# Half-width loads for two FFN weight slices, one PSUM bank for both tokens of a pair, and a new load order

## The chip, the cores and the metric

The kernel runs on one core of a Trainium2 chip. The metric is the device time of one execution in microseconds; of several executions the median is taken. TensorE (PE) does the matrix products and the transposes, VectorE (DVE), ScalarE (ACT) and GpSimd (POOL) do the elementwise work, and SyncE (SP) issues every DMA of this kernel.

## The reference

```python
state = np.zeros((B, H, D, D))            # B=4, H=8, S=768, D=64
for t in range(S):
    state = gamma[None, :, None, None] * state + np.einsum('bhd,bhe->bhde', k[:, :, t], v[:, :, t])
    y[:, :, t] = scale * np.einsum('bhd,bhde->bhe', q[:, :, t], state)
x = y.transpose(0, 2, 1, 3).reshape(B * S, H * D)     # 3072 x 512
h = np.maximum(x @ w_in, 0.0)                         # w_in: 512 x 2048
out = h * h @ w_out                                   # w_out: 2048 x 512, out in float32
```

It is a retention recurrence with one decay per head, followed by a feed-forward network (FFN) with a squared ReLU.

## The kernel before

The 3072 tokens are worked in 24 tiles of 128 tokens, numbered m, six for each batch. For each tile the recurrence is done in chunked form in two halves of 64 tokens ("sub"): scores of k and q (`scores`, L566), sums of k and v (`sums`, L577), a causal mask on DVE (L620), the running state on DVE (L631, L633), then `values` (L540) and `apply` (L555), and a scaled copy into the FFN input `xt` (L642). The decay is folded into tables that scale v and y. A call `visit(m, n)` (L581) issues values and apply of tile m and scores and sums of tile n in one piece on TensorE. In this text "scores n" is the scores and sums of tile n, and "apply m" is values and apply of tile m.

Scores need k and q transposed. Before the change this is done in four ways:

- Tiles 0 to 3 come in pairs (`together`, L397): one DMA of 512 KB for each of k, q and v brings 256 tokens, with neighbouring tokens g = 0 and 1 on one partition. The casts (L411, POOL, ACT or DVE) write bf16 "twins" that lie in an FFN buffer named h. For each g and each of k and q, four transposes (L430) go into a PSUM bank of their own, and one copy takes the bank out for both tiles, into every second column. Rows of k and v are brought into token order by matmuls with a permutation (L449, "placing") and copied out of PSUM.
- Tiles 4 to 6 (below `NPE`) are loaded singly (L470, 256 KB each), cast (L476), and transposed with four 128x128 transposes for each of k and q (L523), which are called a transpose side here.
- Tiles 7 to 9 (`NPE` to `NTD`) are transposed by `flips`, 32 transposes of 64x64 into spare columns of the PSUM tile `yy` (L496), and one copy of 1024 elements on ACT (L502).
- Tiles 10 to 23 are transposed by a DMA that SP issues (L514, called X with the tile's number).

The FFN takes blocks of 1, 2 or 4 tiles (`BLOCKS`). `ffn1` (L663) multiplies with `w_in`, held in four slices of 512 columns, in groups that fill one PSUM bank (L680, 512 columns in all), then ReLU on ACT (L685) and the square on DVE (L690). `ffn2` (L705) multiplies with `w_out`, held in four slices of 512 rows, four matmuls of 512 columns for each slice (L724), then a copy on ACT (L732) and a store of 256 KB on SP (L736). Each weight slice comes in one DMA of 1 MB into one of four float32 buffers `wst` (`weights`, L649), and four casts (L657) on whichever of DVE, ACT and POOL the planner picks write it as bf16. w_out slices reuse the buffers of the w_in slices.

The order of all work on each engine is made ahead of time by a planner (`Plan.schedule`, L65). Each operation is given engines, costs, data it reads and writes, and a priority; the planner puts them down one after the other and chooses the earliest start, then the lowest priority value. The emitted order is fixed: on the chip each engine works through its queue in order, and an instruction that waits holds back what stands behind it. Loads are ranked by the string `ORDER` (L219). Four PSUM banks (`fps`) are handed out by the planner with "open", "use" and "close". It also emits 40 tiny matmuls at the start (`PRE`) and filler matmuls (L776) where it expects TensorE to be idle around `WARM`.

The planner's order of loads before the change, in full up to the weights' end: k0 v0 q0 k2 v2 w_in0 q2 w_in1 q4 w_in2 k4 w_in3 w_out0 k5 w_out1 v4 q5 w_out2 q6 v5 v6 w_out3 q7 k6 k7 v7.

Of the kernel before, what the change touches and what calls it, by code (L numbers as in the profile page):

```python
# [11 lines left out]
BF16 = mybir.dt.bfloat16  # L12
# [6 lines left out]
class Plan:  # L19
# [45 lines left out]
    def schedule(self, nbanks, max_open):  # L65
        ops = self.ops
        n = len(ops)
# [7 lines left out]
        end = [None] * n  # L75
# [10 lines left out]
        bank_free = [0.0] * (nbanks - 1) + [WARM + 1]  # L86
        bank_of = {}
        open_groups = set()
        pipe = made = 0.0
        late = []  # L90
        outstanding = {e: [] for e in eng_free}
# [2 lines left out]
        while done < n:  # L94
            best = None
            for eng, cand in pool.items():
                ef = eng_free[eng]
                for i in cand:
                    o = ops[i]
                    t = max(ef, ready_at[i])  # L100
                    b = o["bank"]
# [69 lines left out]
                eng_free[eng] = t + dur  # L171
                end[i] = t + dur + o["lat"]
            if b is not None and b[0] == "close":
                bank_free[bank_of[b[1]]] = end[i]
                open_groups.discard(b[1])
            if b is not None:
                o["bank_index"] = bank_of[b[1]]
            done += 1
# [9 lines left out]


SMALL = (1.20, 0.93, 65, 0.6)  # L190
TWIN = (1.20, 1.75, 65, 0.6)
TURN = (0.60, 1.10, 16, 2.4)
WIDE = (0.60, 2.80, 33, 0.6)
STORE = (0.30, 0.80, 9, 0.6)
BLOCKS = [2, 1, 1, 1, 1, 2, 4, 2, 2, 4, 4]
SPLIT = 6
AHEAD = 4
WARM = 14.0
FILL = 0.215
WARMING = 5.5  # L200
PACE = 6
LEAD = 2
NPE = 7
NTD = 10
PRE = 40
CVT = {'DVE': 0.69, 'POOL': 1.1}
TCAST = {'DVE': 0.43, 'ACT': 0.63, 'POOL': 0.78}
TEVAC = {'ACT': 0.6, 'DVE': 0.62}
MEVAC = {'ACT': 0.6}
NPAIR = 2  # L210
F2LAG = 3.0
F2WAIT = 4
# [4 lines left out]


ORDER = (  # L219
    "k0 v0 q0 k2 v2 i0 q2 i1 q4 i2 o0 o1 k4 i3 k5 v4 q5 o2 q6 v5 v6 o3 q7 k6 k7 v7"  # L220
)


# [8 lines left out]
def kernel(  # L232
# [164 lines left out]
    def together(n):  # L397


        b, i = where(2 * n)  # L400
        m, s0, w, twin = 2 * n, (2 * n) % NLD, n % 2, twins[n % 2]
        rows_ = lambda x: ld[x][:, s0 : s0 + 2, :].rearrange("s u n -> s (u n)")
        held = lambda x: (f"ld{x}{s0}", f"ld{x}{s0 + 1}")
        for x in "kqv":
            pl.add(f"ld{x}{m}", "SP", TWIN, (), held(x),
                   lambda x=x: nc.sync.dma_start(  # L406
                       rows_(x).rearrange("s (h n) -> s h n", h=H),
                       src[x][b, :, i * C : (i + 2) * C, :].rearrange("h (s g) d -> s h (g d)", g=2)),
                   prio=dma_prio[(x, m)])
        for g in range(2):  # L410
            for x in "kq":  # L411
                o = twin[x][:, g, :].rearrange("s (j a d) -> s a j d", a=2, j=NJ)
                t = rows_(x).rearrange("s (a j g d) -> s a j g d", a=2, j=NJ, g=2)[:, :, :, g, :]
                pl.add(f"c{x}{m}.{g}", TCAST, 0, held(x), (f"twin{x}{w}.{g}",),
                       lambda on, t=t, o=o: copy_on(on, o, t), prio=urgency(m))
            t = rows_("v").rearrange("s (h g d) -> s h g d", h=H, g=2)[:, :, g, :]
            pl.add(f"cv{m}.{g}", CVT, 0, held("v") + ("vf2",), (f"twinv{w}.{g}",),
                   lambda on, t=t, g=g: (nc.vector if on == "DVE" else nc.gpsimd).tensor_tensor(
                       out=twin["v"][:, g, :].rearrange("s (h d) -> s h d", h=H), in0=t,
                       in1=vf2[:, i // 2, g, :, None].to_broadcast([P, H, D]), op=ALU.mult),  # L420
                   prio=urgency(m))
        q0 = m % NQT
        for g in range(2):
            for x, name in enumerate("kq"):
                o1 = {}

                def turn_fn(x=x, name=name, g=g, o1=o1):
                    ps = fps[o1["op"]["bank_index"]].bitcast(BF16)
                    for j in range(NJ):
                        nc.tensor.transpose(ps[:, j * P : j * P + P], twin[name][:, g, j * P : j * P + P], ident[:])  # L430
                i0 = pl.add(f"T{name}{m}.{g}", "PE", 0.26, (f"twin{name}{w}.{g}", "ident"), (f"gT{name}{m}{g}",), turn_fn,
                            prio=-200 + m, lat=0.2, count=4, bank=("open", ("T", m, x, g), False))
                twin_users.append(i0)
                o1["op"] = pl.ops[i0]
                pl.add(f"E{name}{m}.{g}", TEVAC, 0, (f"gT{name}{m}{g}",),
                       (f"qkT{q0}.{name}{g}", f"qkT{q0 + 1}.{name}{g}"),
                       lambda on, x=x, g=g, o1=o1: copy_on(
                           on, qkt_all[:, q0 : q0 + 2, x].rearrange("p c j (t g) -> p c j t g", g=2)[:, :, :, :, g],
                           fps[o1["op"]["bank_index"]].bitcast(BF16)[:, 0:512].rearrange("p (j c t) -> p c j t", j=NJ, c=2)),
                       prio=urgency(m), lat=0.05, bank=("close", ("T", m, x, g)))  # L440
        for c in range(2):
            r = slice(L * c, L * c + L)
            for name in "kv":
                o1 = {}

                def place(name=name, r=r, o1=o1):
                    ps = fps[o1["op"]["bank_index"]]
                    for g in range(2):
                        nc.tensor.matmul(ps[:], lhsT=perm[r, g, :], rhs=twin[name][r, g, :], start=(g == 0), stop=(g == 1))  # L449
                i0 = pl.add(f"N{name}{m + c}", "PE", 0.45, (f"twin{name}{w}.0", f"twin{name}{w}.1", "perm"), (f"gN{name}{m + c}",),  # L450
                            place, prio=-190 + m + c, lat=0.2, count=2, bank=("open", ("N", m + c, name), False))
                twin_users.append(i0)
                o1["op"] = pl.ops[i0]
                o = bf[name][(m + c) % NBF]
                o = o.rearrange("s j a d -> s (j a d)") if name == "k" else o.rearrange("s h d -> s (h d)")
                pl.add(f"M{name}{m + c}", MEVAC, 0, (f"gN{name}{m + c}",), (f"bf{name}{(m + c) % NBF}",),
                       lambda on, o=o, o1=o1: copy_on(on, o, fps[o1["op"]["bank_index"]][:]),
                       prio=urgency(m + c), lat=0.05, bank=("close", ("N", m + c, name)))
# [25 lines left out]
               prio=urgency(m))  # L484

    def qkeys(m):
        return [f"qkT{m % NQT}.{x}{g}" for x in "kq" for g in range(2)]

    def flips(m):

# [15 lines left out]
    def transpose(m):  # L506
# [10 lines left out]
        for x, name in enumerate("kq"):  # L517
            o1 = {}

            def fn(x=x, o1=o1):  # L520
                ps = fps[o1["op"]["bank_index"]].bitcast(BF16)
                for j in range(NJ):
                    nc.tensor.transpose(ps[:, j * P : j * P + P], t[:, x, j].rearrange("s a d -> s (a d)"), ident[:])  # L523
            i0 = pl.add(f"T{name}{m}", "PE", 0.26, (f"bf{name}{m % NBF}", "ident"), (f"gT{name}{m}",), fn,
                        prio=-200 + m, lat=0.2, count=4, bank=("open", ("T", m, x), False))
            o1["op"] = pl.ops[i0]
            pl.add(f"E{name}{m}", EVAC, 0, (f"gT{name}{m}",), qkeys(m)[2 * x : 2 * x + 2],
                   lambda on, x=x, o1=o1: copy_on(on, qkT[:, x].rearrange("p j t -> p (j t)"),
                                                  fps[o1["op"]["bank_index"]].bitcast(BF16)[:, 0:512]),
                   prio=urgency(m), lat=0.05, bank=("close", ("T", m, x)))  # L530
# [115 lines left out]
                   prio=urgency(m))  # L646


    def weights(kind, j):  # L649
        slot = (j if kind == "in" else 4 + j) % NWS  # L650
        st = wst[slot]
        dst = w_in_bf[j] if kind == "in" else w_out_bf[j]
        wv = (moe_w_in.rearrange("(cb p) f -> p cb f", p=P)[:, :, j * 512 : (j + 1) * 512] if kind == "in"
              else moe_w_out.rearrange("(fb p) n -> p fb n", p=P)[:, 4 * j : 4 * j + 4, :])
        pl.add(f"ldw{kind}{j}", "SP", WIDE, (), (f"wst{slot}",),
               lambda: nc.sync.dma_start(st[:], wv), prio=dma_prio[(kind, j)])  # L656
        for c in range(4):  # L657
            pl.add(f"cw{kind}{j}.{c}", WCAST, 0, (f"wst{slot}",), (f"w{kind}{j}.{c}",),
                   lambda on, c=c: copy_on(on, dst[:, c, :], st[:, c, :]),
                   prio=WPRIO[kind] + j)  # L660


    def ffn1(blk):  # L663
# [5 lines left out]
        for f0 in range(0, NFB, per):  # L669
            grp = ("f1", blk, f0)  # L670
            j = f0 // 4
            reads = [f"xt{g % NXT}.{u0 + u}" for u in range(nb)] + [f"win{j}.{cb}" for cb in range(NCB)]
            o1 = {}

            def mm(f0=f0, j=j, o1=o1):
# [29 lines left out]
    def ffn2(blk):  # L705
        for q4 in range(blk0[blk], blk0[blk] + blocks[blk]):
# [5 lines left out]
            for part in range(parts):  # L712
# [2 lines left out]
                keys = [f"osb{slot}.{part}"] if parts > 1 else [f"osb{slot}.0", f"osb{slot}.1"]  # L715
                o1 = {}
                for j in range(4):
                    reads = [f"h{g % NH2}.{u}.{4 * j + c}" for c in range(4)] + [f"wout{j}.{c}" for c in range(4)]

                    def mm(j=j, o1=o1, h2=h2, u=u, ns=ns, w=w):  # L720
                        ps = fps[o1["op"]["bank_index"]]
# [16 lines left out]

    dma_prio = {x: n for n, x in enumerate(dma_order(NM))}
    urgency = lambda m: m - 3.0  # L740
    for j in range(4):
        weights("in", j)
    for j in range(4):
        weights("out", j)
    done = done2 = 0
    for m in range(-1, NM):
        n = m + 1
# [62 lines left out]
```

## Time and profile before

| what | value |
|---|---|
| median of 4 runs | 213.54 us (213.42 to 213.6) |
| the profiled execution | 213.49 us, span 211.6 us |
| mean granted TensorE clock | 0.992 |
| busy: PE, DVE, ACT, POOL | 200.4, 113.6, 94.5, 42.6 us |
| FFN input product (L680), FFN output product (L724) | 93.9 and 92.4 us busy |
| DMA moved | 37.64 MB, mean 178 GB/s |
| w_in slice, w_out slice, from issue to landing | 9.8 and 9.3 us (median) |

The span is the time from the first to the last instruction; the execution's own time is longer by what lies around it. Busy times of different engines overlap. The row of tenths on the page cuts the span into 40 slices of 5.29 us. Queries of the trace give the same execution in order of time; in brackets stands how long the engine sat idle before an instruction and what released it. When a load has landed is read from the first cast that it released.

### The profile page before, as it was taken

How to read it: one execution, taken by the hardware profiler on the slowest of the kernel's cores; microseconds unless marked ns; L12 is line 12 of the kernel's file. 1: busy time of each engine (PE TensorE's matmuls, PEld its weight loads, DVE VectorE, ACT ScalarE, POOL GpSimd, SP SyncE). 2: the span in 40 equal slices, each digit the busy share in tenths (PEclk: the TensorE clock that was granted, in tenths of full speed). 3: DMA queues.
4: the chain of work that ended last, by engine and by line, in shares of the span. 5: the costliest groups of instructions: out<-in, count | busy, mean ns of one | idle time of the engine just before them, and what ended most of it. 6: DMA issues, size and time to landing. Idle time of an engine off the chain costs nothing.

```text
span 211.6 us, 6380 instructions
## 1 busy us (share of the span) xinstructions
PE 200.4 (95%) x2788; PEld 119.1 (56%) x2788; DVE 113.6 (54%) x253; ACT 94.5 (45%) x157; POOL 42.6 (20%) x70
## 2 busy tenths in 40 slices
PE   2886999999999999999999999999999999999994
PEld 2344888675676755444566667644444444444453
DVE  3465889765577764367863753656463442322100
ACT  8675666544355521265334244223534324534321
POOL 6551423305233231232322121310000000000000
PEclk9997899999999999999999999999999999999999
DMA  6999999999999996999999999981011011011022
GB/s 166 290 343 343 348 352 247 296 299 201 264 233 205 215 224 156 253 203 230 156 240 203 210 245 201 235 181 63 0 53 50 3 50 50 3 51 50 0 102 99
DMA packets 91276, 37.64 MB, mean 178 GB/s; under 512 B 77808, under 2 KB 84208, under 8 KB 91248
## 3 DMA queue, kind: packets, MB, share of 16 engines
q1 hardware_dynamic: 91248, 37.23, 76.7%
q8 instruction: 22, 0.36, 0.7%
q14 instruction: 6, 0.05, 0.1%
HBM read 27.26 MB, written 6.29 MB: 159 GB/s over the span
## 4 chain that ended last, share of the span: by engine, by line
PE 88%; DMA 5%; SPq 3%; ACT 1%; DVE 1%; issue 0%
PE fps L680 40%; PE fps L724 38%; DMA qn<-in_q_dram 5%; SPq L406 3%; PE yy L540 2%; PE yy L555 2%; PE sc L566 2%; PE sc L577 1%; ACT qkT L502 1%; SPq L656 1%; PE fps L523 1%; DVE xt L642 1%; PE yy L496 1%; PE fps L430 0%; ACT h L388 0%
## 5 line engine op out<-in xcount | busy, mean ns | idle before, releaser
L680 PE MATMUL fps<-xt,w_in 128*128 128x256 bf16 (+2 forms) x704 | 93.9, 284 | 0.1
L724 PE MATMUL fps<-w_out,h 128*128 128x512 bf16 (+1 forms) x400 | 92.4, 371 | 0.0
L685 ACT ACTIVATE h<-fps 128x512 bf16<-128x512 f32 x96 | 57.2, 597 | 66.5 <-PE fps L680 66.3
L680 PEld LDWEIGHTS <-w_in 128*128 128x128 bf16 x704 | 58.6, 99 | 31.1 <-issue 0.7
L690 DVE TENSOR_TENSOR h<-h 128x512 bf16<-128x512 bf16 x96 | 42.0, 445 | 52.5 <-ACT h L685 51.9
L724 PEld LDWEIGHTS <-h 128*128 128x128 bf16 x400 | 37.5, 98 | 36.0
L732 ACT ACTIVATE osb<-fps 128x512 f32<-128x512 f32 (+1 forms) x25 | 14.5, 580 | 32.2 <-PE fps L724 28.6
L642 DVE TENSOR_TENSOR xt<-yy,yf 128x512 bf16<-128x512 f32 x24 | 16.5, 688 | 17.2 <-PE yy L555 12.8
L392 POOL CAST kqs<-kn 128x512 bf16<-128x512 f32 x19 | 13.0, 687 | 54.4 <-DMA kn<-in_k_dram 44.5
L620 DVE TENSOR_TENSOR pt<-sc,cmask 128x512 bf16<-128x512 f32 x24 | 16.4, 682 | 2.2 <-PE sc L577 2.2
L633 DVE TENSOR_TENSOR state<-sc,state 128x256 bf16<-128x256 f32 x40 | 16.8, 419 | 0.6
L392 POOL CAST kqs<-qn 128x512 bf16<-128x512 f32 x20 | 13.3, 666 | 15.0 <-DMA qn<-in_q_dram 14.9
L481 DVE TENSOR_TENSOR vs<-vn,vf 128x512 bf16<-128x512 f32 x20 | 14.1, 706 | 0.8 <-DMA vn<-in_v_dram 0.8
L555 PE MATMUL yy<-qkT,state 64*64 64x64 bf16 x352 | 12.1, 198 | 0.8 <-DVE state L633 0.3
L540 PEld LDWEIGHTS <-vs 64*64 64x64 bf16 x384 | 5.1, 107 | 7.5 <-issue 7.3
L430 PE MATMUL fps<-ident,h 128*128 128x128 bf16 x32 | 3.9, 284 | 5.2 <-DVE h L390 3.5
L555 PEld LDWEIGHTS <-state 64*64 64x64 bf16 x352 | 7.4, 106 | 1.6 <-PE yy L555 1.1
L540 PE MATMUL yy<-pt,vs 64*64 64x64 bf16 x384 | 7.6, 197 | 0.6 <-DVE pt L620 0.6
L566 PE MATMUL sc<-qkT 64*64 64x64 bf16 x384 | 7.7, 198 | 0.0
L577 PE MATMUL sc<-vs,kqs 64*64 64x64 bf16 x352 | 7.7, 196 | 0.0
L388 ACT ACTIVATE qkT<-fps 128x512 bf16<-128x512 bf16 x7 | 4.8, 698 | 5.6 <-PE fps L523 3.5
L390 DVE COPY qkT<-fps 128x512 bf16<-128x512 bf16 x7 | 3.9, 557 | 6.0 <-PE fps L430 2.6
(54 smaller groups left out, 77.4 us busy)
## 6 DMA issues: line engine op xcount, KB each, us to landing
out_dram<-osb SPq DMA_DIRECT2D x23, 256.0 KB, 2.9
qn<-in_q_dram SPq DMA_DIRECT2D x20, 256.0 KB, 5.1
kn<-in_k_dram SPq DMA_DIRECT2D x20, 256.0 KB, 5.3
vn<-in_v_dram SPq DMA_DIRECT2D x20, 256.0 KB, 5.2
wst<-in_moe_w_in_dram SPq DMA_DIRECT2D x4, 1024.0 KB, 9.8
wst<-in_moe_w_out_dram SPq DMA_DIRECT2D x4, 1024.0 KB, 9.3
kn<-in_k_dram SPq DMA_DIRECT2D x2, 512.0 KB, 5.7
vn<-in_v_dram SPq DMA_DIRECT2D x2, 512.0 KB, 6.4
```

The costliest lines, as they stand in the source:

```text
L392: nc.gpsimd.tensor_copy(o, t)
L481: lambda: nc.vector.tensor_tensor(out=o[:], in0=t.rearrange("s (h d) -> s h d", h=H), in1=vf[:, i, :, None].to_broadcast([P, H, D]), op=AL ...
L540: nc.tensor.matmul(yy[L * c : L * c + L, sub, p * L : p * L + L], lhsT=vs[r, 4 * a + j, :], rhs=pt[r, a, j, :], start=(p == 0), stop=True, ...
L555: nc.tensor.matmul(yy[L * c : L * c + L, sub, p * L : p * L + L], lhsT=st[r, j, :], rhs=qkT[r, 1, j, sub * L : sub * L + L], start=False, ...
L620: lambda: nc.vector.tensor_tensor(out=pt[:], in0=sc[:, :, 0:256].rearrange("s g (p t) -> s g p t", p=NJ), in1=cmask[:, None, None, :].to_b ...
L633: f = lambda cc=cc, j1=j1, j0=j0: nc.vector.tensor_tensor(out=sts[j1][:], in0=cc, in1=sts[j0][:], op=ALU.add)
L642: lambda: nc.vector.tensor_tensor(out=xt[:, :, u * C : u * C + C].rearrange("s p (g t) -> s g p t", g=2), in0=yy[:, :, 0:256].rearrange("s ...
L680: nc.tensor.matmul(ps[:, u * n : u * n + n], lhsT=w_in_bf[j][:, cb, c * P : (c + 1) * P], rhs=xt[:, cb, cols], start=(cb == 0), stop=(cb = ...
L685: nc.scalar.activation(h2[:, f0 : f0 + per, cols], ps[:].rearrange("p (u n) -> p u n", u=per), AF.Relu)
L690: nc.vector.tensor_mul(hv, hv, hv)
L724: nc.tensor.matmul(ps[:, 0:w], lhsT=h2[:, fb, u * C : u * C + C], rhs=w_out_bf[j][:, c, ns], start=(fb == 0), stop=(fb == NFB - 1))
L732: lambda o1=o1, slot=slot, ns=ns, w=w: nc.scalar.activation(osbs[slot][:, ns], fps[o1["op"]["bank_index"]][:, 0:w], AF.Copy),
```

## The change

- The first two slices of `w_in` are loaded in two DMAs each, of 256 columns (512 KB), and each half is cast by two instructions of 128 x (2 x 256). The data names carry the half, so that an FFN group can begin when the half it reads is cast. The other six slices stay whole.
- Both tokens g of a pair are transposed into one PSUM bank, g = 0 in the first 512 columns of bf16 and g = 1 behind it. Two copies take the bank out, one for each tile; each reads both g. The planner learns banks that close after two operations.
- The copies of the pairs' transposes and the pairs' k and q casts lose DVE as a choice; the copies of the placings gain it.
- `NPE = NTD = 8`: tiles 4 to 7 are transposed by TensorE in the manner of L523, no tile by flips, tiles 8 to 23 by DMA.
- `BLOCKS`, `ORDER`, `PRE`, `WARM` and a cost are set anew.

The planner's order of loads after the change: k0 v0 q0 v2 k2 q2, both halves of w_in0, both halves of w_in1, q4 w_in2 v4 w_in3 w_out0 k4 w_out1 k5 w_out2 w_out3 v5 q5 k6 v6 q6 q7 v7, store 0, k7 k8 q8, store 1, v8 k9 q9, store 2, X8 v9 k10 q10 X9. On TensorE, from scores 2 on: scores 2, two groups of block 0 (w_in0), apply 2, scores 3, two groups (w_in1), q4's transposes, one group of block 1, apply 3, one group of block 1, then groups on w_in2 and the first group of block 2.

```diff
-TWIN = (1.20, 1.75, 65, 0.6)
+TWIN = (1.20, 1.80, 65, 0.6)
-BLOCKS = [2, 1, 1, 1, 1, 2, 4, 2, 2, 4, 4]
+BLOCKS = [2, 1, 1, 1, 1, 2, 2, 2, 4, 4, 4]
-WARM = 14.0
+WARM = 16.0
-NPE = 7
-NTD = 10
-PRE = 40
+NPE = 8
+NTD = 8
+PRE = 20
+WHALF = 2
+WHALFD = (0.60, 1.47, 33, 0.6)
-TCAST = {'DVE': 0.43, 'ACT': 0.63, 'POOL': 0.78}
-TEVAC = {'ACT': 0.6, 'DVE': 0.62}
-MEVAC = {'ACT': 0.6}
+TCAST = {'ACT': 0.63, 'POOL': 0.78}
+TEVAC = {'ACT': 0.6}
+MEVAC = {'ACT': 0.6, 'DVE': 0.62}
-    "k0 v0 q0 k2 v2 i0 q2 i1 q4 i2 o0 o1 k4 i3 k5 v4 q5 o2 q6 v5 v6 o3 q7 k6 k7 v7"
+    "o0 k0 v0 o1 q0 v2 k2 o2 q2 o3 i0 i1 i2 i3 q4 i4 v4 i5 k4 k5 v5 q5 k6 v6 q6 q7 v7 k7"
...
-        for g in range(2):
-            for x, name in enumerate("kq"):
+        for x, name in enumerate("kq"):
...
+                    nc.tensor.transpose(ps[:, 512 * g + j * P : 512 * g + j * P + P],
+                                        twin[name][:, g, j * P : j * P + P], ident[:])
...
+            for c in range(2):
+                pl.add(f"E{name}{m}.{c}", TEVAC, 0,
+                       [f"gT{name}{m}{g}" for g in range(2)], [f"qkT{q0 + c}.{name}"],
+                       lambda on, x=x, c=c, o1=o1: copy_on(
+                           on, qkts[q0 + c][:, x].rearrange("p j (t g) -> p j t g", g=2),
+                           fps[o1["op"]["bank_index"]].bitcast(BF16).rearrange("p (g j c t) -> p c j t g", g=2, j=NJ, c=2)[:, c]),
+                       prio=urgency(m + c), lat=0.05, bank=("close", ("T", m, x), 2))
...
+    pieces = {"in": [(j, h, 2) for j in range(WHALF) for h in range(2)] + [(j, 0, 1) for j in range(WHALF, 4)],
+              "out": [(j, 0, 1) for j in range(4)]}
+
+    def weights(kind, n):
+        j, half, parts = pieces[kind][n]
...
+        pl.add(f"ldw{kind}{n}", "SP", WHALFD if parts == 2 else WIDE, (), held,
+               lambda: nc.sync.dma_start(st, wv), prio=dma_prio[(kind, n)])
+        for c in range(0, 4, parts):
...
+                   lambda on, c=c: copy_on(on, dst[:, c : c + parts], st[:, c : c + parts]),
+                   prio=WPRIO[kind] + j)
```

## The prediction

> **What bounds the kernel now.** I read the page first: how busy each engine is, the granted clock, the chain.
>
> ```profile
> PE 200.4 (95%) x2788; PEld 119.1 (56%) x2788; DVE 113.6 (54%) x253; ACT 94.5 (45%) x157; POOL 42.6 (20%) x70
> ...
> PEclk9997899999999999999999999999999999999999
> ...
> PE 88%; DMA 5%; SPq 3%; ACT 1%; DVE 1%; issue 0%
> ```
>
> TensorE is the bound: 95% busy, 88% of the chain. The rest of the chain is DMA and its issue, and the clock sags only in slices 4 and 5 (16 to 26 us). So I looked for the place where TensorE isn't yet bound, in the chain in order of time (start, length, what):
>
> ```profile
> 8.40 9.66 DMA qn<-in_q_dram
> 18.08 0.64 ACT h L388
> 18.77 1.01 PE fps L430 x8
> 19.78 1.71 PE fps L680 x8
> ...
> 28.64 0.22 PE fps L523 x4
> 28.86 6.19 PE fps L680 x88
> ```
>
> The second pair's q lands at 18.06; its transposes stand in TensorE's queue ahead of the first FFN group, which starts at 19.78. From there TensorE has no gap above 0.1 us. The windows of one microsecond show what the wait for q costs besides:
>
> ```profile
> 16.00:17.00 1.00, 0.61 (x32) 0.39 (x31) 0.96 (x3) 0.52 (x2) 0.00 (x0) 1.00 1.00 365
> 17.00:18.00 1.00, 0.16 (x8) 0.05 (x8) 0.69 (x1) 0.00 (x0) 0.00 (x0) 1.00 1.05 391
> 18.00:19.00 1.00, 0.23 (x3) 0.24 (x4) 0.00 (x0) 0.92 (x2) 0.61 (x1) 0.91 1.12 330
> 19.00:20.00 1.00, 1.00 (x10) 0.87 (x8) 0.18 (x1) 0.81 (x2) 0.00 (x0) 0.50 1.27 274
> ```
>
> Columns: window, its length, busy time of PE, PEld, DVE, ACT, POOL, then clock, DMA share, GB/s. TensorE worked little from 15.3 to 18.8, then its clock is 0.5 to 22.9: over 18 to 23 the missing clock adds to 1.7 us. DMA is full all the while. How close the weights follow is in POOL's timeline (start, length, ... idle before, released by); every cast starts as its slice lands:
>
> ```profile
> 14.91 0.61 POOL L392 CAST w_in<-wst 128x512 bf16<-128x512 f32 x1 [0.70 <-DMA wst<-in_moe_w_in_dram]
> ...
> 20.93 0.87 POOL L392 CAST w_in<-wst 128x512 bf16<-128x512 f32 x1 [2.20 <-DMA wst<-in_moe_w_in_dram]
> ...
> 24.91 0.61 POOL L392 CAST w_in<-wst 128x512 bf16<-128x512 f32 x1 [2.26 <-DMA wst<-in_moe_w_in_dram]
> ...
> 28.62 0.68 POOL L392 CAST w_in<-wst 128x512 bf16<-128x512 f32 x1 [2.08 <-DMA wst<-in_moe_w_in_dram]
> 31.42 1.55 POOL L392 CAST w_out<-wst 128x512 bf16<-128x512 f32 x2 [2.12 <-DMA wst<-in_moe_w_out_dram]
> ...
> 40.19 0.61 POOL L392 CAST w_out<-wst 128x512 bf16<-128x512 f32 x1 [2.26 <-DMA wst<-in_moe_w_out_dram]
> ...
> 47.69 0.87 POOL L392 CAST w_out<-wst 128x512 bf16<-128x512 f32 x1 [5.47 <-DMA wst<-in_moe_w_out_dram]
> ```
>
> w_in3 is cast by 30.3 and used at 31.5 (28.86 plus three of the seven groups in 6.19 us, 0.88 each); w_out3 is cast by 48.6 and used at 48.87. So up to 49 us TensorE runs only 0.3 to 2 us behind the loads: an earlier start is paid out only as far as the loads allow.
>
> **The change, part by part.** Group prices at full clock: FFN1 0.88 us (above), FFN2 0.86 (chain row of four L724), one side's transposes 0.22, scores and sums 0.37.
>
> *Load order.* v, k and q of the second pair now come before any weight: q moves ahead of 1 MB. Pair loads land 1.8 us apart (k0 4.9, q0 8.5, k2 10.4, v2 12.2), so q lands at about 14.0, not 18.06. The first half of w_in0 lands at 15.4 (before, the whole at 14.9), the second at 16.9, the halves of w_in1 at 18.4 and 19.9. In the profile everything from that q on lands 1.4 us later than this spacing gives (14.9 + 1.8 = 16.7 against 18.06); I let it hit w_in1 (19.7, 21.2) and all after it.
>
> *Halves.* Rows of 1 KB instead of 2. DMA moved 290 GB/s with 512-byte rows (6 to 11 us) and 380 with 2 KB (12 to 14 us). A fixed time per row between these two puts 1 KB near 347, 1.51 us a half against 1.36: 0.6 us over the four. [...] Bounds 0 and 1.4 (as slow as 512-byte rows). The cast work is unchanged: two instructions of 512 elements per half, DVE 0.42, ACT 0.62, POOL 0.65.
>
> *Start, walked through the new queues.* Both casts of the first k are on POOL: its second transposes start 0.7 us later, hidden, since scores 0 wait for q at 8.5. Two tokens in one bank: as many transposes (32) and evacuations (8); each now reads both tokens but serves one tile, so scores 0 need one of them: 11.3 instead of 11.57. Then, with the rows' durations: POOL scales v2 10.4 to 11.6 (1.21), scores 0 end 11.9, v2's placing (0.62) 12.5; k2's casts 12.2 to 12.85, first transposes to 13.2; DVE masks scores 0 and makes two states (0.69 + 2 x 0.42) 12.0 to 13.45; apply 0 13.25 to 13.75; scores 1, waiting for the states, 13.75 to 14.35; k's other transposes and a placing to 15.0; q (cast 14.0 to 14.7) transposed 15.0 to 15.9. DVE meanwhile makes x of tile 0 from 13.85, masks scores 1, makes two states, to 15.95: apply 1 runs 15.9 to 16.5. New head-of-line waits: ACT casts w_in0's first half (lands 15.4) ahead of evacuating q, so scores 2 start at 16.8; DVE casts w_in0's second half (16.9 to 17.35) ahead of x of tile 1 (0.7), so the first FFN group starts at 18.1; and DVE casts a half of w_in1 (19.7) ahead of masking tile 2's scores, so apply 2 waits until 20.9. Scores 3 follow tile 2's states (21.6) and end at 22.0. Then TensorE is fed: two groups on w_in1 to 23.75, q4's transposes 24.0, one group 24.9, apply 3 25.4, one group 26.3, four more on w_in2 (cast by 26.3) and w_in0 to 29.9. The next needs w_in3: landed 29.2, DVE's two casts and one each on ACT and POOL end by 30.2.
>
> Before reached this group at 31.5, having done one transpose side more (0.22) and one FFN1 group fewer (0.88). Lead: 31.5 - 30.2 + 0.88 - 0.22 = 2.0 us.
>
> *Clock.* The emptiest 3.4 us in the new queue is 17.3 to 20.9 with 1.75 busy; before it was 15.3 to 18.8 with 1.2, and that cost 1.7 us. [...] I take 0, being nearer to the work of 10 to 15 us, at clock 1.00.
>
> *FFN output weights and tile 5.* w_out2 and w_out3 now come before most of tiles 5 to 7. Spacing 2.8 per slice and 1.1 per small load (the rows before: q6 41.4, v5 42.55, v6 43.6) gives w_out1 36.0, w_out2 39.9, w_out3 42.7, v5 43.8, q5 44.85. The queue from 30.2: four groups 33.75, one FFN2 group 34.6, k4 34.85, two groups 36.65, scores 4 37.0, FFN2 on w_out1 37.9, k5 38.1, FFN2 39.0, apply 4 39.5, FFN2 40.4. First group on w_out2 wanted at 40.4, possible at 40.8; on w_out3 wanted at 43.45, possible at 43.6; q5's transposes wanted at 45.4, possible at 45.5. Scores 5 end at 48.1. Before, the same set was done at 49.73 (48.87 plus one FFN2 group). Lead: 1.6 us.
>
> *Flips against transposes.* Tiles 7 to 9 lose their flips (three rows of 0.38 in the chain, 1.14 us of TensorE); tile 7 gets two transpose sides instead (0.44). Saved: 0.7 us, all on the path, as TensorE is full. Tiles 8 and 9 now go by DMA transposes on SP, 4.6 us to landing (3.6 to 6.1), none on TensorE. X8 stands behind store 2 and q8's cast: about 55.5, landing 60; scores 8 are wanted at 63. X9 follows X8 and three loads: about 61.5, landing 66; wanted at 67.4. Cost taken 0; bounds 0 and 4 us.
>
> *At nothing:* 20 fewer starting matmuls and three more fillers (TensorE is idle there; without that cover 0.1 us each). BLOCKS gives the same counts of 1, 2 and 4 tiles, so FFN work is equal; it only wants tiles 10 and 11 later. Evacuations moved between ACT and DVE (54% and 45% busy).
>
> *Sum.* 1.6 + 0.7 = 2.3 us. Profiled execution 213.49, span 211.6, so 1.89 outside; 209.3 + 1.89 = 211.2. The median of the runs, 213.54, is 0.05 above it.
>
> **The rivals.**
> *Late w_out3.* Before it landed 4.1 us after v6, 1.3 more than a slice takes. If so here, its group waits 1.45 us and the lead at scores 5 falls to 0.2 to 0.5: gain 1.0, 212.5. For it: the same row. Against: it need not fall on this load.
> *Clock falls.* It costs 1.7 before 30 us, of which later waits (0.7) give back part: gain 1.2, 212.3.
> *Loads without the 1.4 us.* All waits shrink; gain 3.6, 209.9.
> *Nothing left:* both late loads and clock: 213.4.
> *Slower: X9 decides.* A DMA transpose is in SP's queue and TensorE waits in order. From a landing after 67.4 every microsecond counts, and from 69.7 the change loses. With a landing at 71 it costs 3.6: 213.5 - 2.3 + 3.6 = 214.8. For it: the slack is about 1.4 us, where before tile 10's transpose left 2.4, and DMA is full. Against: landing was never above 6.1 us.
>
> **How the numbers follow.** Main case 0.47 (210.5 to 211.9), early loads 0.09, late w_out3 0.18, clock 0.10, nothing left 0.04, slower 0.12. About 0.2% (0.4 us) is what a measurement of this kernel can tell from no change. Faster: 0.47 + 0.09 + 0.10 + 0.16 of the late case = 0.82; same 0.04 + 0.02 = 0.06; slower 0.12. The range 209.9 to 213.3 leaves out half of the early case and the slower one.
>
> **What would show it.** Right: q's cast near 14, first FFN group near 18, no clock of 0.5 there, w_in3's casts near 29.2, first group on it near 30.2, about 1 us of gaps between 36 and 46, no L496 rows, no gap before scores 8 and 9. Wrong: a first FFN group after 19.5, w_in3 after 30, a gap of over 1 us near 43 or 67, a second stretch of half clock.

## The result and the profile after

| | before | after |
|---|---|---|
| median | 213.54 us (63 runs, 212.9 to 214.85) | 212.68 us (42 runs, 211.6 to 213.98) |
| ratio, after to before | | 0.9954 (95% interval 0.9942 to 0.9966) |
| profiled execution; span | 213.49; 211.6 us | 212.27; 210.5 us |
| mean granted clock in it | 0.992 | 1.000 |
| last matmul of the program ends | 208.54 us | 207.24 us |

The kernel is faster by 0.46%, 1.0 us by the ratio: the forecast direction, inside the range, but less than half of the forecast 2.3 us. The question is where the other 1.3 us went.

The page after, with the lines that answer to the first three of before (busy time, granted clock by slices, chain):

```profile
PE 198.7 (94%) x2683; PEld 118.0 (56%) x2683; DVE 114.8 (55%) x253; ACT 90.8 (43%) x154; POOL 43.0 (20%) x72
...
PEclk9999999999999999999999999999999999999999
...
PE 92%; DMA 3%; issue 1%; SPq 1%; POOL 1%; ACT 0%
```

The fall of the clock is gone in this execution, TensorE has a larger share of the chain, and 1% of the chain is "issue", time in which an engine waited for nothing that the profile shows. Before it was 0%. First, did the loads do what was forecast? POOL's timeline, after (start, length, what, idle before and its releaser):

```profile
13.98 0.61 POOL L397 CAST h<-qn 128x512 bf16<-128x512 f32 x1 [1.17 <-DMA qn<-in_q_dram]
15.49 0.61 POOL L397 CAST w_in<-wst 128x512 bf16<-128x512 f32 x1 [0.89 <-DMA wst<-in_moe_w_in_dram]
16.99 0.61 POOL L397 CAST w_in<-wst 128x512 bf16<-128x512 f32 x1 [0.89 <-DMA wst<-in_moe_w_in_dram]
19.66 0.87 POOL L397 CAST w_in<-wst 128x512 bf16<-128x512 f32 x1 [2.06 <-DMA wst<-in_moe_w_in_dram]
...
29.16 0.61 POOL L397 CAST w_in<-wst 128x512 bf16<-128x512 f32 x1 [3.23 <-DMA wst<-in_moe_w_in_dram]
...
42.47 0.87 POOL L397 CAST w_out<-wst 128x512 bf16<-128x512 f32 x1 [2.13 <-DMA wst<-in_moe_w_out_dram]
```

They did: q at 13.98 (forecast 14.0), the halves at 15.5, 17.0 and 19.7, w_in3 at 29.16 (29.2), w_out3 at 42.5 (42.7), q5 at 44.6 (44.85). The data are there. TensorE isn't. Its chain in order of time (start, length, what):

```profile
18.07 0.10 PE sc L587 x12
18.17 1.21 issue
19.38 0.22 PE sc L587 x4
19.60 1.85 PE fps L699 x16
...
25.33 0.18 PE yy L550 x8
25.51 0.88 issue
26.39 0.26 PE yy L550 x8
```

Scores 2 are done and sums 2 (L587) have begun. After 12 of its 16 matmuls TensorE stands still for 1.21 us, and after 8 of the 16 of values 3 (L550) for 0.88 us. Both stops are in the middle of a series, and the trace names no engine and no load that released them. The first FFN group starts at 19.53 instead of 18.1; a start after 19.5 was one of the signs that the prediction had named for being wrong.

### The profile page after: what moved, and what is told of

Its sections match the earlier page's. It is cut to its first block, busy times and chain, and to the rows that moved or that the text cites. A ratio compares the mean times of both kernels' runs of the same rounds, so it can differ in the third digit from the quotient of the medians.

```text
span 210.5 us, 6166 instructions
## 1 busy us (share of the span) xinstructions
PE 198.7 (94%) x2683; PEld 118.0 (56%) x2683; DVE 114.8 (55%) x253; ACT 90.8 (43%) x154; POOL 43.0 (20%) x72
## 4 chain that ended last, share of the span: by engine, by line
PE 92%; DMA 3%; issue 1%; SPq 1%; POOL 1%; ACT 0%
PE fps L743 40%; PE fps L699 40%; DMA vn<-in_v_dram 3%; PE yy L550 3%; PE yy L565 2%; PE sc L587 2%; PE sc L576 2%; SPq L411 1%; PE fps L459 1%; PE fps L533 1%; POOL h L423 1%; PE fps L434 1%; PE fps L794 0%; ACT osb L751 0%
## 5 line engine op out<-in xcount | busy, mean ns | idle before, releaser
L699 PE MATMUL fps<-xt,w_in 128*128 128x128 bf16 (+2 forms) x704 | 92.4, 282 | 0.0
L709 DVE TENSOR_TENSOR h<-h 128x512 bf16<-128x512 bf16 x96 | 43.5, 461 | 52.8 <-ACT h L704 52.6
L652 DVE TENSOR_TENSOR xt<-yy,yf 128x512 bf16<-128x512 f32 x24 | 16.4, 684 | 14.9 <-PE yy L565 14.9
L397 POOL CAST kqs<-qn 128x512 bf16<-128x512 f32 x20 | 13.5, 675 | 11.3 <-DMA qn<-in_q_dram 11.2
L565 PE MATMUL yy<-qkT,state 64*64 64x64 bf16 x352 | 12.0, 198 | 0.5
L550 PEld LDWEIGHTS <-vs 64*64 64x64 bf16 x384 | 5.1, 108 | 8.8 <-issue 8.6
L393 ACT ACTIVATE qkT<-fps 128x512 bf16<-128x512 bf16 x12 | 6.7, 596 | 5.2 <-PE fps L533 3.1
L587 PE MATMUL sc<-vs,kqs 64*64 64x64 bf16 x352 | 7.8, 195 | 1.2 <-issue 1.2
L550 PE MATMUL yy<-pt,vs 64*64 64x64 bf16 x384 | 7.9, 200 | 0.9 <-issue 0.9
L565 PEld LDWEIGHTS <-state 64*64 64x64 bf16 x352 | 7.4, 107 | 1.1 <-PE yy L565 1.1
L587 PEld LDWEIGHTS <-kqs 64*64 64x64 bf16 x352 | 5.6, 109 | 1.3 <-issue 1.3
```

Of the source, the lines that this page charges most:

```text
L397: nc.gpsimd.tensor_copy(o, t)
L550: nc.tensor.matmul(yy[L * c : L * c + L, sub, p * L : p * L + L], lhsT=vs[r, 4 * a + j, :], rhs=pt[r, a, j, :], start=(p == 0), stop=True, ...
L565: nc.tensor.matmul(yy[L * c : L * c + L, sub, p * L : p * L + L], lhsT=st[r, j, :], rhs=qkT[r, 1, j, sub * L : sub * L + L], start=False, ...
L587: nc.tensor.matmul(sc[L * a : L * a + L, sub, 256 + j * D : 256 + j * D + D], lhsT=ks[r, j, a, :], rhs=vs[r, 4 * a + j, :], start=False, s ...
L652: lambda: nc.vector.tensor_tensor(out=xt[:, :, u * C : u * C + C].rearrange("s p (g t) -> s g p t", g=2), in0=yy[:, :, 0:256].rearrange("s ...
L699: nc.tensor.matmul(ps[:, u * n : u * n + n], lhsT=w_in_bf[j][:, cb, c * P : (c + 1) * P], rhs=xt[:, cb, cols], start=(cb == 0), stop=(cb = ...
```

## The experiments

**Two theories.** By the first, TensorE waits for its own instructions. On the page the number of packets in a DMA queue of kind "instruction" goes with TensorE's work: TensorE has 2683 matmuls and as many weight loads after, and 5366 / 256 = 21.0, where 256 is the distance between the two stops that is counted below; before it is 5576 / 256 = 21.8. The row after (packets, MB, share of 16 engines' time):

```profile
q8 instruction: 21, 0.34, 0.7%
```

Before, the same row has 22 packets. These quotients are a hint and no more: the first packet in the span turns out below to bring instruction 450, so the last one reaches beyond the last matmul. In bytes, 0.34 MB in 21 packets is about 16 KB each. Counted in TensorE's queue, 223 matmuls have run before the first stop and 351 before the second. With their weight loads and the three semaphore and drain instructions that the trace has ahead of them, the stops stand at instruction 450 and at 706, 256 apart. By the second theory a wait for data or a semaphore, that the trace doesn't name, sits at these two places. They part when instructions are added or taken away at the head of the queue: the first lets the stops move by just so many instructions, the second leaves them where they are. The starting matmuls (`PRE`, 20 after, 40 before) read constants and nobody reads their results, so they serve for that. In most runs their number alone is changed, where they are issued, so that the planner's order stays.

**No starting matmuls.**

```diff
-            for _ in range(PRE):
+            for _ in range(0):
```

> The changed kernel, but none of its 20 starting matmuls is emitted (the planner still counts them, so every other instruction keeps its place). TensorE's instructions 450 and 706, before which it waited 1.21 and 0.88 us for nothing that the profile names, become old instructions 490 and 746: the end of the first two FFN groups, and a block of FFN groups. Theory 1 (TensorE waits for the next block of 256 instructions, and the wait shows when the 50 or so instructions ahead of the block's end are short ones): both waits vanish or stay below 0.3 us, the first FFN group starts near 18.3, the first group on w_in3 near 30.3, time about 1.3 us below the changed kernel, near 211.3. Theory 2 (the waits are for data or a semaphore that the profile doesn't name, at those two places in the work): both waits stay where they stand, in scores 2 and values 3, time 212.6.

Measured: 213.14 us (211.68 to 214.25, 12 runs), ratio 0.9965 (0.9932 to 0.9998). The stop in sums 2 is gone and the first FFN group starts at 18.50. The second stop moved on by 40 instructions, from values 3 into apply 3 (L565), after 12 of its 16 matmuls. The expectation had put this point into an FFN group, which was wrong. TensorE's timeline:

```profile
25.34 0.54 PE L565 MATMUL yy<-qkT,state 64*64 64x64 bf16 x12
26.91 0.22 PE L565 MATMUL yy<-qkT,state 64*64 64x64 bf16 x4 [1.03 <-issue]
```

This is where the count of instructions has it: 351 matmuls have run, and no data are late there. No time was won: the FFN group behind apply 3 starts at 27.13 by the chain (after: 27.05), since the one remaining stop takes back what the first gave.

**Thirty.** The same edit with `range(30)`.

> The changed kernel with 30 starting matmuls emitted in place of 20: the two places move 20 instructions up the queue, to old 430 (sums 2) and old 686 (inside the first group of block 1, behind 1.9 us of FFN groups). Theory 1: the first wait stays, at the start of sums 2, about 1 us; the second vanishes; time 0.3 to 0.9 below the changed kernel, near 212.0. Theory 2: both waits stay in scores 2 and values 3, 212.6.

Measured: 212.32 us (211.29 to 213.59, 8 runs), ratio 0.9931 (0.9899 to 0.9964). The first stop, 1.09 us, moved forward by the 20 instructions, to after 2 matmuls of sums 2; the second is gone, as instruction 706 now lies in FFN work. The second theory has fallen.

**Before, with 76.** `range(PRE)` becomes `range(76)` in the kernel before. This puts instruction 706 of the old queue into scores 3.

> The kernel before with 76 starting matmuls in place of 40, all in time in which TensorE is idle (up to 5.4 us). Instructions 450 and 706 become old 378 (values 1, ahead of the wait for the second q) and old 634 (between scores 3 and sums 3, with only values, apply and scores, about 0.7 us, ahead of it). Theory 1: a new wait of about 1 us in scores 3 near 25, and one near 16 that the wait for q hides; time 0.5 to 1.2 us above before, near 214.4. Theory 2: no new wait, 213.5.

Measured: 214.62 us (213.5 to 216.02, 12 runs), ratio 1.0049 (1.0022 to 1.0076): slower, but with no stop in scores 3. The expectation missed. The trace shows why: the packet for instruction 706 starts at 19.6, and TensorE, which waits for q here too, comes to that instruction only at 24.9, 5.2 us later. What else differs from before is in the loads. w_in0 lands at 16.47 instead of 14.91, and late in the start-up w_out3 at 48.2 instead of 47.7. TensorE waits for w_out3, as the chain shows:

```profile
48.22 0.88 POOL w_out L392
49.14 1.02 PE fps L724 x4
```

The last matmul ends 0.64 us later (209.18). Why w_out3 is late is not settled; that of w_in0 is taken up below.

**The order of loads alone.** The kernel before with the new `ORDER` string; whole slices, two banks, flips and 40 starting matmuls stay.

```diff
-    "k0 v0 q0 k2 v2 i0 q2 i1 q4 i2 o0 o1 k4 i3 k5 v4 q5 o2 q6 v5 v6 o3 q7 k6 k7 v7"
+    "k0 v0 q0 v2 k2 q2 i0 i1 q4 i2 v4 i3 o0 k4 o1 k5 o2 o3 v5 q5 k6 v6 q6 q7 v7 k7"
```

> The kernel before with the changed kernel's order of loads alone: whole slices, a bank for each token, flips for tiles 7 to 9. The prediction's sum would give: q near 14, w_in0 near 16.9, w_in3 0.6 earlier than with halves (28.6), the lead of about 2 us at w_in3 without the 0.7 of the flips: 1.3 to 1.8 below before. Theory 1: instructions 450 and 706 stand in scores 2 and in values 3, as in the changed kernel, so waits of about 1 us each come here too, and the time is 0 to 0.7 below before, near 213.2. Theory 2: the halves make the waits, so none here, near 212.

Measured: 213.07 us (212.82 to 213.59, 12 runs), ratio 0.9968 (0.9946 to 0.999), 0.7 us of the 1.0. One stop of 0.65 us in scores 2 (17.6 to 18.26), which the kernel before doesn't have: earlier data alone bring it about. The second one, expected in values 3, did not come: TensorE met that place at 25.0, 2.5 us behind its packet. The first FFN group starts at 19.23.

**Fillers against stops and clock.** Matmuls of 256 columns into an unread part of `yy` were put ahead of the first FFN group and of apply 2: six and six with no starting matmuls, and in a second kernel six and four with 5 starting matmuls and 15 matmuls of one column. They were meant to keep TensorE's clock up, which is the third theory: that falls of the clock set the median. In the second kernel slow instructions stand right around the block's end.

```diff
+                for _ in range({"F1.0.0": 6, "V2.": 6}.get(o["name"], 0)):
+                    nc.tensor.matmul(yy[:, 0, 256:512], lhsT=ident[:],
+                                     rhs=ident[:, None, :].to_broadcast([P, 2, P]), start=True, stop=True,
+                                     skip_group_check=True)
```

> The kernel of e1 (no starting matmuls) with six filler matmuls of 256 columns ahead of the first FFN group and six ahead of apply 2, written to columns that nothing reads. In e1 TensorE was idle there for 0.70 and 0.64 us, and its twelve times fell into two groups, 211.7 to 212.4 and 213.9 to 214.3. Theory 3 (the median is set by whether the idle places around 17 to 21 us let the clock fall for a stretch of about 3.4 us): with the places filled the upper group vanishes, median near 212.1, granted clock near 1.0 in the profile. Theory 1 alone (only the wait for instructions costs): the fillers change nothing, half of the times stay near 214. The wait at instruction 706 now stands at the start of apply 3, about 1 us, by both.

> As e5, but five starting matmuls, six and four fillers, and 15 matmuls of one column ahead of apply 2, so that instruction 450 stands in the first two FFN groups and 706 in the first group of block 1, both behind slow instructions. Theories 1 and 3 together: no wait for instructions, no fall of the clock, first FFN group near 18.5, first group on w_in3 near 30.5, TensorE's end 1.0 to 1.5 us earlier than in the profile of the changed kernel; median near 211.2, which is what the prediction's sum gave. Rival (after 30 us the loads bind, so that nothing of it arrives): 212.0 with new gaps between 40 and 46 us.

Measured: 212.34 us (212.27 to 212.8, 6 runs), ratio 0.9939 (0.9916 to 0.9961), and 212.51 us (211.84 to 212.71, 6 runs), ratio 0.9938 (0.9914 to 0.9961). The first still has its stop of 1.14 us at instruction 706, in apply 3. The second was to be free of stops and isn't: 0.33 us at 19.9 and 0.73 us at 26.64, both inside FFN groups. Slow instructions right ahead did not help; these stops too end 2.5 to 2.7 us behind the start of a packet (below). In both, the mean clock was 0.998 or higher in every run, and the times near 214 of the kernel without starting matmuls did not come in these six. The third theory fits that; the run with 40 and fillers, below, does not fit it.

**Flips back.** `NPE = 7`, `NTD = 10` as before the change, all else as after.

> The changed kernel with flips for tiles 7 to 9 as before and DMA transposes from tile 10; TensorE's queue is the same up to the weights. By the prediction's sum the flips cost 1.14 us of TensorE and the transposes of tile 7 cost 0.44: 0.7 us above the changed kernel, near 213.3. Rival (hidden): no difference.

Measured: 212.84 us (212.2 to 214.9, 12 runs), ratio 0.9974 (0.9945 to 1.0003): by the ratios 0.0020 above after, 0.4 us, with intervals that overlap; its lowest run lies 0.6 us above after's lowest (211.6). Up to the flips its queue is that of after, and yet the stop in sums 2 took 2.41 us in its profile (an execution of 214.9 us, with the clock at half from 18.8 to 25.6), where after has 1.21: TensorE came to it 0.67 us earlier, and the packet 0.5 us later. The stop's place is fixed, its size is not.

**Whole slices.** `WHALF = 0`, and in `ORDER` the text `i0 i1 i2 i3 q4 i4 v4 i5` becomes `i0 i1 q4 i2 v4 i3`, which is the same order of data.

> The changed kernel with whole slices of w_in (i0 i1 q4 i2 v4 i3 in the order of loads). Instructions 450 and 706 stand in sums 2 and values 3 as in the changed kernel, so both waits should stay. By the prediction's step the halves delay w_in3 by 0.6 us and bring the first group's half 1.4 us earlier than a whole slice: whole, the first group starts within 0.3 us of 19.5, since the wait for instructions and q stand before it anyway, and w_in3 lands near 28.6; time within 0.4 of the changed kernel. If the halves carry the gain: 0.5 or more above it.

Measured: 212.56 us (212.47 to 212.59, 7 runs), ratio 0.9943 (0.9923 to 0.9964). No difference from after in the time: the halves bring nothing that can be measured, nor do they cost it, though w_out0 lands 0.6 us earlier with whole slices (31.28 against 31.91). Of the two waits that were expected the first is there, with 1.69 us. The second isn't: the clock is at half from 19.2 to 22.7 in this profile, and TensorE comes to instruction 706 at 26.6, 3.5 us behind its packet.

**Forty.** If instruction 450 is met before anything is late and 706 in FFN work, both stops should be nearly gone. With `range(40)` in after they stand in scores 2 and in the FFN.

> The changed kernel with 40 starting matmuls emitted in place of 20. The runs so far suggest that a block of 256 instructions of TensorE reaches it 5 to 7 us after it began on the block before (changed kernel: began 14.05, next at 19.38; then 19.38 and 26.39). Here the first such block begins at scores 0 (11.9), so instruction 450, in scores 2 near 17.8, should be there by 17.0 to 18.4, and 706, in the first group of block 1 near 24.6, by about 25. Theory 1: both waits shrink to 0 to 0.5 us, the first FFN group starts near 18.5, lowest times near 211.2. Theory 3: the idle 0.7 us before the first group and 0.6 before apply 2 remain as in e1, so times still spread over 2 us. Theory 2: waits as in the changed kernel.

Measured: 212.41 us (211.27 to 213.96, 12 runs), ratio 0.993 (0.9903 to 0.9956). What TensorE waited for:

```profile
PE fps L699 <- DVE xt L652: 0.8, 1, 0.8
PE sc L576 <- issue: 0.3, 1, 0.3
```

The second stop is gone and 0.27 us is left of the first. The profiled execution took 211.31 us, span 209.5; its last matmul ends at 206.32, 0.9 earlier than after. Windows of two microseconds, first of after, then of this kernel (length, busy time of PE, PEld, DVE, ACT, POOL, clock, DMA share, GB/s):

```profile
18.00:20.00 2.00, 0.79 (x33) 0.60 (x18) 0.85 (x3) 0.53 (x2) 0.34 (x1) 1.00 1.17 315
...
24.00:26.00 2.00, 1.51 (x30) 1.28 (x28) 1.97 (x5) 1.72 (x4) 0.69 (x1) 1.00 1.07 339
```

```profile
18.00:20.00 2.00, 0.97 (x37) 0.80 (x30) 1.06 (x3) 0.62 (x2) 0.88 (x2) 1.00 1.17 316
...
24.00:26.00 2.00, 1.92 (x57) 1.65 (x55) 1.97 (x6) 1.76 (x4) 0.52 (x1) 1.00 1.09 335
```

From 24 us on TensorE is now nearly full. From 18 to 20 it isn't, for another reason: w_in0's second half is there at 18.43 (after: 16.99), and its cast stands ahead of x of tile 1 in DVE's queue, the head-of-line wait that the prediction named, with a later load:

```profile
18.43 0.43 DVE L395 CAST w_in<-wst 128x512 bf16<-128x512 f32 x1 [0.80 <-DMA wst<-in_moe_w_in_dram]
18.77 0.68 DVE L652 TENSOR_TENSOR xt<-yy,yf 128x512 bf16<-128x512 f32 x1
```

So the first FFN group starts no earlier than in after (19.51 against 19.53). What was won was won at the second stop: the FFN group behind apply 3 starts at 25.87, where after has 26.98.

```profile
19.51 1.91 PE L699 MATMUL fps<-xt,w_in 128*128 128x256 bf16 x16 [0.76 <-DVE xt L652]
...
25.87 2.38 PE L699 MATMUL fps<-xt,w_in 128*128 128x128 bf16 x28
```

**Forty with fillers.** Four and four fillers as above.

> As e9 with four fillers each ahead of the first FFN group and of apply 2, 0.43 us of work in places that are idle for 0.6 to 0.7. Theories 1 and 3 together: waits below 0.5, no fall of the clock, times within 0.6 us of each other, median near 211.5, the lowest of all kernels here. If the fillers cost what they fill: 212.0.

Measured: 213.12 us (211.83 to 215.03, 12 runs), ratio 0.9965 (0.9931 to 0.9999). No stop, but the fillers themselves waited 1.03 us for x of tile 1 and held the first FFN group until 19.96. Mean clocks of 0.984 to 0.992 appear here too: fillers are no cure for the falls of the clock.

**Sixty-six.** This puts instruction 706 near the end of sums 3, to bring a stop back on purpose.

> The changed kernel with 66 starting matmuls. The block begins at 11.4, so instruction 450, at the start of apply 1 near 16.75, waits 0 to 1.1 us; instruction 706, near the end of sums 3 at about 22.4, is only some 5.5 us behind it and should wait about 1.5 us, at a place where neither the changed kernel nor any other here waits. Theory 2: no wait at sums 3.

Measured: 212.01 us (211.71 to 212.03, 4 runs), ratio 0.991 (0.9875 to 0.9945). The stop came where it was called for, after 14 of the 16 matmuls of sums 3, with 1.05 us (22.03 to 23.09).

**The packets themselves.** DMA's view of a short window gives the packets of a queue that started in it: number, MB, and the time they took as a share of 16 engines' time. After, the window 16.8 to 16.9 us:

```profile
q8 instruction: 1, 0.02, 67.9%
```

67.9% of 16 times 0.1 us is 1.09 us for one packet. Nine stops, with the packet read in this way (it starts within 0.1 us of the time given; the kernels are named by their number of starting matmuls or their edit):

| kernel, stop | packet starts | takes | TensorE goes on | since the packet's start |
|---|---|---|---|---|
| after, sums 2 | 16.8 | 1.1 | 19.38 | 2.6 |
| after, values 3 | 23.6 | 1.2 | 26.39 | 2.8 |
| none, apply 3 | 24.1 | 1.3 | 26.91 | 2.8 |
| 30, sums 2 | 15.8 | 1.2 | 18.38 | 2.6 |
| order alone, scores 2 | 15.8 | 1.1 | 18.26 | 2.5 |
| flips back, sums 2 | 17.3 | 1.1 | 19.91 | 2.6 |
| whole slices, sums 2 | 16.4 | 1.1 | 19.00 | 2.6 |
| 40, scores 2 | 15.8 | 1.2 | 18.37 | 2.6 |
| 66, sums 3 | 20.3 | 1.3 | 23.09 | 2.8 |

The three stops of the kernels with fillers end 2.5 to 2.7 us behind theirs. So each stop ends 2.5 to 2.8 us after a packet began, and each stands where exactly 223 or 351 matmuls have run: the packet is what TensorE waited for. In after it began 2.8 and 4.2 us after TensorE had started on the block before (14.05 and 19.38), so a block of 256 takes 5.3 and 7.0 us to follow, while TensorE was through the first of these blocks in 4.1 us. In all thirteen kernels the first two packets begin 1.5 to 4.3 us after TensorE has begun on the block before. Before, the packets started at 15.5 and 22.9; with 2.6 us they are usable at 18.1 and 25.5, and TensorE, waiting for q, reached these places at 21.5 and 26.4. That is why the kernel before shows nothing of it.

The first packet also goes with a late load. After, w_in1's first half lands 2.7 us behind the half before it, where the two halves before lie 1.5 apart (packet at 16.8); with 40 the late one is w_in0's second half, 2.9 behind (packet at 15.8); with 66 w_in0's first, at 16.66 instead of 15.49 (packet at 12.9); before, with 76, w_in0 at 16.47 instead of 14.91 (packet at 11.4, before at 15.5). These runs differ from after or before in the starting matmuls alone, and the delay, 0.9 to 1.5 us beyond the usual spacing in the thirteen kernels, moves with the first packet from load to load. This is the 1.4 us that the prediction found behind q in the old profile and carried over as a property of the loads: by luck it hit the load that it was assigned to. Later packets don't do the same: after, those at 23.6, 30.3 and 37.4 us last as long, and the slices around them follow at their usual 2.7 to 2.9 us. Why the first packet goes with a late load and the later ones don't, no run here shows; the cause stays open.

## Why the prediction was right in direction and too large

- *Load order, halves.* Right: every load within 0.4 us. The halves follow 1.50 us apart (forecast 1.51), and their price is small (whole slices measure the same). That the four halves cost 0.6 us of DMA time was an estimate from two rates, 290 and 380 GB/s; the landings that it led to came out (w_in2 25.24, w_in3 29.16, w_out0 31.91), and with whole slices w_out0 landed 0.63 us earlier. That the "1.4 us later" goes with an instruction packet was not known; that it came at the forecast place is luck.
- *The start, walked through the queues.* Scores 0 came at 11.32 (forecast 11.3), scores 2 at 17.8 (16.8). Apply 0 was 0.8 late already (14.0 instead of 13.25), behind a placing of 1.04 us where the walk had 0.62, since TensorE's matmuls took about twice their later time until about 14 us (see below); later, one placing (0.53) and two fillers (0.22) stand in the chain that the walk did not have. "The first FFN group starts at 18.1" was 19.53. Without starting matmuls, and so without the first stop, it is 18.50: the walk itself was off by 0.4 and the stop cost 1.03. The second stop followed before apply 3. The first group on w_in3, forecast for 30.2, came at 31.46 (27.05 and five groups), with w_in3 cast by 30.94: TensorE was late there, not the weights. Before reached this group at 31.5, so of the forecast lead of 2.0 us only 0.7 is left, and that by the transpose side and group (0.88 less 0.22) that are ordered otherwise.
- *FFN output weights and tile 5.* The landings were right; the "about 1 us of gaps between 36 and 46" is absent because TensorE came late anyway. Scores 5 end at 49.0 (forecast 48.1): lead 0.73 instead of 1.6 us. This is the term of the sum that was mis-sized. With 40 starting matmuls they end at 48.2, a lead of 1.5, and q5's transposes start at 45.46, where the prediction had them possible at 45.5: without the second stop this step of the sum nearly comes out.
- *Flips against transposes.* Right: forecast 0.7; from 49 us to the end of TensorE's work the lead grows by 0.57 (208.54 less 207.24 is 1.30, less 0.73), and putting the flips back costs 0.4 by the ratios. X8 and X9 cost nothing: no gap stands before scores 8 and 9, and the rival that made the kernel slower did not come.
- *At nothing.* This is the failing step. "20 fewer starting matmuls" were costed at their own run time, which idle time hides. Each is also two places in the queue: their number decides which instruction is the first of a block. With 20 it falls into sums 2 and values 3, runs of short matmuls, and the stops there took 1.21 and 0.88 us. With 40 it falls into scores 2, where 0.27 us is left, and into FFN work, and the profiled execution takes 211.31 us, against the forecast 211.2. The walk had a term for data, for engines and for queues, and none for TensorE's own instructions. The profile before had no such stop to show, but it had the row of 22 instruction packets.
- *Clock.* Taken as 0. In 19 of the 43 executions of after, the profiled one among them, the mean clock was 0.997 or more; their median is 212.12 us, though they reach from 211.6 to 213.97. In 19 others it was 0.990 to 0.992, with a median of 212.72. So of the 1.5 us between 211.2 and 212.68, some 0.6 go with the clock, and 0.9 are there without a fall too. In the runs of the kernel before beside these experiments the same two groups lie at 213.2 and 213.5, so it has the falls as well. The prediction's window was misread: from 15.3 to 18.8 the old kernel's TensorE worked 0.92 us, not 1.2, with no idle stretch above 1.6 us, and from 17.3 to 20.9 the new one's worked 2.39, not 1.75. The 0 rested on this comparison alone; no run shows how full a stretch must be for the clock to hold, nor that a stretch of 3.4 us is what counts. The rest of the spread without a fall stays open.

The traces say more of the clock than the prediction took from them. Its "clock 1.00" of the work of 10 to 15 us is in part no measured clock: the clock's record begins only at 12.0 us before and at 14.3 after, and the views count the time ahead of it as 1.00. The same transposes take about twice as long there. Before, eight of them:

```profile
9.44 1.31 PE L430 MATMUL fps<-ident,h 128*128 128x128 bf16 x8
...
12.11 0.62 PE L430 MATMUL fps<-ident,h 128*128 128x128 bf16 x8
```

After, four and then eight:

```profile
13.38 0.63 PE L434 MATMUL fps<-ident,h 128*128 128x128 bf16 x4
...
15.81 0.62 PE L434 MATMUL fps<-ident,h 128*128 128x128 bf16 x8
```

So one of these transposes took 0.16 us ahead of the record and 0.08 in it. In the five profiles with a fall (before, with and without 76, 30, flips back, whole slices) the record begins at 11.9 to 12.4 us, and the fall follows 6.8 us behind it, at 18.8 to 19.3, for 3.4 us (flips back 6.8). In the eight without a fall it begins at 12.8 to 15.0. So in these thirteen executions an early beginning and a fall go together; what sets either, no run shows.

In the profiled execution the gain is 1.22 us, 1.1 short of the sum. The lead at scores 5 is 0.87 below forecast (1.6 less 0.73), the flips 0.13, and the tail behind the last matmul is 0.2 longer (3.26 against 3.06); what lies outside the span gives 0.12 back (1.77 against 1.89). That the stops are worth those 0.9 us is shown by the profiled execution with 40: its last matmul ends 0.92 earlier than that of after, and the time was won at the second stop. Its median is only 0.3 below after's, and the two intervals overlap, since 6 of its 12 runs have the lower clock (median 212.54); the other 6 have 211.45, where after has 212.12. This version and those with 30 and 66 beat the kernel before with their whole intervals; that they beat after isn't settled by so few runs. So in single executions the cause is shown; how much of the median it explains is not.

## What to carry to other kernels

When a change lets data come earlier, ask what feeds the engine besides data. In a stretch of short instructions beside busy DMA (a share of 1.04 to 1.17 from 14 to 28 us here), count the instructions: in this kernel TensorE was through 256 in less than the 5 to 7 us that the next 256 took to follow, and stood still in the middle of a series. The stops that the trace puts down to "issue" moved by exactly the number of instructions taken away or added ahead of them (40 for 20 starting matmuls, 20 for 10), and that told them from a wait for data. Twenty more starting matmuls moved them to places where 0.27 us was left of the first stop's 1.21 and nothing of the second's 0.88.

## What the runs showed of the hardware

- TensorE's instructions came in packets of about 16 KB (after, 21 with 0.34 MB), and the stops stood at instructions 450 and 706, 256 apart (matmul and weight load one each). The packets of the stops took 1.1 to 1.3 us (after, at a DMA share of 1.04 to 1.17), and TensorE went on 2.5 to 2.8 us after their start. The first two packets began 1.5 to 4.3 us after TensorE had begun on the block before.
- In all thirteen kernels one load behind the span's first instruction packet landed 0.9 to 1.5 us later than its spacing; with the packet moved by starting matmuls alone, it was another load. The packets between 20 and 38 us delayed none by more than 0.4 us.
- Executions of one kernel differed in mean clock: of 43 of after, 19 had 0.997 to 1.0, 19 had 0.990 to 0.992 and 5 had 0.984, with medians of 212.12, 212.72 and 213.84 us. In the five profiles with a fall it began 6.8 us after the start of the clock's record and lasted 3.4 us, once 6.8. TensorE was not idle ahead of it: before, it was busy for 0.92 us of the 3.5 from 15.3 to 18.8. After, with 2.39 us busy of the 3.6 from 17.3 to 20.9, the clock stayed at 1.00 in the profiled execution.
